# Attention and a gated MLP on one core: float32 scores for the first block alone, float16 pairs for the second block of the first batch

## The chip, the cores and the metric

One core of a Trainium2 chip runs the whole program. The metric is the device time of one execution in microseconds (us). The kernel before took 637.03 us, the median of three runs (636.49 to 640.52). One further execution was taken by the profiler; all rows come from it.

## The reference

```
scores = q @ k.T / 8, causal mask          q, k, v: 4 batches, 12 heads, 448 tokens, head size 64
attn = softmax(scores)                      (denominator + 1e-9)
x = (attn @ v), heads side by side          1792 tokens x 768
h = x @ w_in                                w_in 768 x 2048
g = h * sigmoid(1.702 h)
out = g @ w_out                             w_out 2048 x 768, everything float32
```

The inputs q and k are scaled up so that scores are far from flat, and the result has float32 accuracy. A single float16 operand isn't enough for that.

## The kernel before, in words

**Float16 pairs.** Nearly every product is made with operands split in two float16 numbers, a high part (`scaled`, L476 on ACT or L478 on DVE) and the rest (`rest`, L481, always DVE). A product is then three or four float16 matmuls that add up in PSUM. The weights come in as the high words of wider numbers: `to_f32` (L570 to L603) puts float32 together, then `split` makes the pairs (L476, L481). w_in goes through `w_in_slice` in 8 slices into `wib`, w_out through `w_out_load` and `w_out_split` in 16 pieces into `wob`.

**Blocks.** Each batch has 7 chunks of 64 tokens, cut in two blocks: chunks 0 to 3 and chunks 4 to 6. The 8 blocks are numbered n = 0 to 7; n = 0 and n = 1 belong to batch 0. A block has 6 units, a unit is two heads. `unit` makes the scores of each chunk (`scores_of`), the masked row maximum (L1091, DVE), the exponential with its row sum (L1105, ACT), reciprocal and pairs of probabilities (`p_pair`), one DMA transpose of them (L1179), the product with the values (L1197, PE) and, for two units, the pairs of the result in `xT` (L476, L481). Then `moe` takes the block: `h_slice` (L1268, PE, `xT` by `wib`, the gate on ACT and DVE into `gT`) and `out_tile` (L1333, PE, `gT` by `wob`). The out projection of n = 0 needs every piece of `wob` (16 splits at L481 on DVE).

**Two ways to scores.** `f32(b, u)` chooses. In batch 0 all units (`nf` is 6) take float32: `k_unit32` loads the keys of two heads of the block alone, `turn` transposes them on PE against an identity (L870), one copy brings them from PSUM to `kT`; `q_unit32` does the same for the queries, with two copies into `qT`; `scores32` issues one float32 matmul for a chunk, which the trace shows as two (L1060). Batches 1 to 3 take pairs: `k_pair` loads all 448 keys of four heads, takes a sum of squares (L466, ACT), the maximum over the partitions (`all_max`: L430 on PE, L632 on DVE), a power of two for scale (`norm_scale`: L443 on DVE, L450 and L457 on POOL or DVE), high part and rest into `k16`, and one DMA transpose into `kT` (L961). `q_pair` does this for the queries of four heads of a block, with sums for each partition alone, and doubles both parts (L1024, POOL); `q_unit` transposes a unit's half by DMA (L1040). `scores` issues four float16 matmuls for a chunk (L1068), each on half of the columns of the array, and L1091 then takes a scale from a column instead of a constant.

**Order.** Every step is handed to `Ops.add` with the engines that can take it, its costs, what it reads and writes, and a due time. `Ops.order` draws 300 variants of a list schedule for the whole kernel with a fixed seed, keeps the best by its own costs, and issues the instructions of each engine in that order. Loads and transposes all go through SP's queue. `keys_values` queues the keys and values of a batch two units ahead of the block that uses them.

Of the kernel before, what the change touches and what calls it, by code (L numbers as in the profile page):

```python
# [26 lines left out]
TUNE = dict(  # L27
    large=2,
    raw=(['W11', 'W11', 'V1', 'V1', 'W13', 'W15', 'W9', 'V0'], ['W11', 'W13', 'W15', 'V1', 'W15', 'V0', 'V0', 'V1']),
    tiny=True,  # L30
    win=(2, 4),
    slack=5.13,
    cuts={0: (0, 4, 7), 1: (0, 4, 7), 2: (0, 4, 7), 3: (0, 4, 7)},
    wi=(-21.7, 11.6),
    wo=(38.54, 116.08),
# [6 lines left out]
    dk=16.55,  # L42
# [2 lines left out]
    tr=26.06,  # L45
    gram_i=True,
    gram_o=False,
    nf=6,
    gram_v=True,
    va=2,  # L50
    ub=(0.0, 60.0, 122.92, 9.75),
# [8 lines left out]
class Ops:  # L60
# [24 lines left out]
    def add(self, costs, fn, r=(), w=(), prio=0.0, dma=0.0, narrow=False):  # L85
        deps = set()
        for key in r:
            if key in self.wrote:
                deps.add(self.wrote[key])
        for key in w:  # L90
            if key in self.wrote:
                deps.add(self.wrote[key])
            deps.update(self.read.get(key, ()))
        me = len(self.ops)
        for key in r:
            self.read.setdefault(key, []).append(me)
        for key in w:
            self.wrote[key] = me
            self.read[key] = []
        deps.discard(me)  # L100
        self.ops.append((costs, fn, sorted(deps), prio, dma, narrow))
# [202 lines left out]
def act(n, psum=False, ap=0, acc=0, rate=0.833):  # L304
    return {"ACT": (rate * n + (52 if psum else 94) + 93 * (ap + acc)) / 1e3}


def dve(n, ap=0, rate=1.042):
    return {"DVE": (rate * n + 68 + 61 * ap) / 1e3}
# [12 lines left out]
def kernel(  # L322
# [14 lines left out]
    NU = H // 2  # L337
# [12 lines left out]
    NB = len(blocks)  # L350
# [43 lines left out]
    add = ops.add  # L394
# [4 lines left out]
    def col(tag, n=2, w=1):  # L399
        if tag not in col_at:  # L400
            col_at[tag] = (col_used[0], Ring(n))
            col_used[0] += n * w
            assert col_used[0] <= 175
        o, ring = col_at[tag]
        i = ring.next()
        return cols[:, o + i * w : o + (i + 1) * w], ("col", tag, i)
# [424 lines left out]

    def f32(b, u):
        return b == 0 and u < TUNE["nf"]

    ident = cp.tile([P, P], F32, name="ident")
    ident_keys = ["ident"]
# [6 lines left out]
            out=ident, in_=ident, pattern=[[-1, P]], compare_op=ALU.is_equal, fill=0.0, base=0, channel_multiplier=1  # L845
        )

    if TUNE["nf"]:
        add({"POOL": 1.0}, identity, [], ident_keys, -1e6)

    def load_heads(dst, src, r, keys, prio, dma):

# [73 lines left out]
    def k_pair(b, u, prio):  # L926

        st = bst[b]
        n = 2 * S
        keys = []  # L930
        for a in range(2):
            for j in range(2):
                keys += [("kf", a, j)]
                add(
                    {"SP": Ops.LOAD},
                    lambda e, a=a, j=j: nc.sync.dma_start(
                        out=kf[64 * j : 64 * j + 64, a], in_=k[b, 2 * (u + a) + j].rearrange("(c p) d -> p c d", p=64)
                    ),
                    [], keys[-1:], prio, dma=0.64,
                )  # L940
        sq, sq_key = col("sqk", 2)
        flat = k16.rearrange("p u c g d -> p (u c g d)")
        junk_k = flat[:, :n].bitcast(BF16).rearrange("p (u c d) -> p u c d", u=2, d=D)
        square_sum(n, junk_k, [("k16", g) for g in range(2)], kf, keys, sq, sq_key, prio)
        amx, amx_key = all_max(sq, sq_key, "k", "S", prio)
        (s, s_key), (inv, inv_key) = col("s_k", 2), col("i_k", 8)
        norm_scale("k", amx, amx_key, s, s_key, inv, inv_key, prio)
        add(
            {**act(n, ap=1), **dve(n, ap=1, rate=0.521)},
            lambda e: scaled(e, k16[:, :, :, 0], kf, s),  # L950
            keys + [s_key], [("k16", 0)], prio,
        )
        add(
            dve(n, ap=1),
            lambda e: rest(k16[:, :, :, 1], kf, s, k16[:, :, :, 0]),
            keys + [s_key, ("k16", 0)], [("k16", 1)], prio,
        )
        t = kT[u // 2]
        add(
            Ops.turned(2 * NC),  # L960
            lambda e: nc.sync.dma_start_transpose(out=t, in_=flat),  # L961
            [("k16", 0), ("k16", 1)], [("kT", u + a, c) for a in range(2) for c in range(NC)], prio - TUNE["tr"], dma=2 * NC * Ops.ROWS,
        )
        for a in range(2):
            st["kT", u + a] = t[:, a * NC : a * NC + NC]
            st["ik", u + a] = inv, inv_key
# [61 lines left out]

    def q_unit(n, u, prio):
        b, c0, c1 = blocks[n]  # L1030
        if f32(b, u):
            return q_unit32(n, u, prio)
        ni = c1 - c0
        if u % 2 == 0:
            q_pair(n, u, prio)
        t, m = qT_r.next(), u % 2
        stale[t] = True
        add(
            Ops.turned(2 * ni),
            lambda e: nc.sync.dma_start_transpose(out=qT[t][:, : 2 * ni], in_=q16[:, m * 256 * ni : (m + 1) * 256 * ni]),  # L1040
            [("q16", m, g) for g in range(4)], [("qT", t)], prio - TUNE["tr"], dma=2 * Ops.ROWS * ni,
        )
        return (qT[t][:, : 2 * ni].rearrange("p (c g) t -> p g c t", g=2), ("qT", t)) + bst[b]["c", n]
# [4 lines left out]
    def scores_of(n, u, run, qt, qt_key, prio):  # L1048

        b, c0, c1 = blocks[n]  # L1050
        kt, kt_keys = bst[b]["kT", u], [("kT", u, x) for x in range(run[-1] + 1)]
        sb = ps_s_r.next()
        places, o = [], 0
        for i in run:
            places.append(ps_s[sb][:, o : o + 64 * (i + 1)])
            o += 64 * (i + 1)

        def scores32(e):
            for i, ps in zip(run, places):
                nc.tensor.matmul(  # L1060
                    ps, qt[:, i - c0].rearrange("p j w -> p (j w)"), kt[:, : 64 * (i + 1)], start=True, stop=True
                )

        def scores(e):
            for i, ps in zip(run, places):
                for g in range(2):
                    for j in range(2):
                        nc.tensor.matmul(  # L1068
                            ps[64 * j : 64 * j + 64],
                            qt[:, g, i - c0, 64 * j : 64 * j + 64],  # L1070
                            kt[:, : i + 1, 64 * j : 64 * j + 64],
                            start=(g == 0),
                            stop=(g == 1),
                        )

        if f32(b, u):
            add({"PE": (4 * o / 2.4 + 150 * len(run)) / 1e3}, scores32, [qt_key] + kt_keys, bank(sb), prio)
        else:
            add(
                {"PE": 2 * (o / 2.4 + 17 * len(run)) / 1e3}, scores, [qt_key] + kt_keys, bank(sb), prio, narrow=True  # L1080
            )
        return [(ps, [("S", sb, x)] if run[1:] else bank(sb)) for x, ps in enumerate(places)]
# [299 lines left out]
    def at(n, u):  # L1382
        p0, p1, p2, d = TUNE["ub"]
        return p0 + d * u if n == 0 else p1 + d * u if n == 1 else p2 + 10.0 * (NU * (n - 2) + u)

    AHEAD = 2

    def keys_values(n, u):
        b, c0, _ = blocks[n]
        if c0:  # L1390
            return
        if b and u == 0:
            v_batch(b, at(n, 0) - 4)
        if u % 2 == 0:
            if not f32(b, u):
                k_pair(b, u, at(n, u) - TUNE["dk"])
            v_pair(b, u, at(n, u) - (TUNE["dv"] if b else TUNE["dv0"]))

    zero_v(-1e6)
    for n, (b, c0, c1) in enumerate(blocks):  # L1400
        if c0 == 0:
            if b == 0:
                for s in range(TUNE["va"]):
                    w_in_slice(s, wi_at(s))
                v_batch(0, TUNE["v0"])
        for u in range(NU):
            if f32(b, u):
                k_unit32(u, c0, c1, at(n, u) - TUNE["dk"])
            if b == 0 and c0 == 0:
                keys_values(n, u)  # L1410
            elif n + (u + AHEAD) // NU < NB:

                keys_values(n + (u + AHEAD) // NU, (u + AHEAD) % NU)
            unit(n, u, at(n, u))
        if n == 0:
            for s in range(TUNE["va"], NWS):
                w_in_slice(s, wi_at(s))
            for nh in range(2):
                for c in range(NWS):
                    w_out_load(nh * NWS + c, TUNE["wo"][nh] + TUNE["wo1"][nh] * c)  # L1420
                w_out_scale(nh, TUNE["wo"][nh] + TUNE["wo1"][nh] * NWS)
            zero_v(TUNE["wo"][1] + TUNE["wo1"][1] * NWS)
        if n:
            moe(n - 1)
# [37 lines left out]
```

## Time and profile before

| | before |
|---|---|
| median of three runs | 637.03 us |
| the profiled execution | 634.5 us |
| its span, first to last instruction | 632.8 us |
| PE, DVE, ACT, POOL busy | 576.9, 420.2, 373.0, 98.6 us |
| matmuls | 5627 |
| mean granted TensorE clock, as a share of 2.4 GHz | 0.97 |

Busy times are averages over very different stretches. The profile has views by stretch (windows), by line and shape of tile, by what a wait was ended by, and a chain of waits that is followed back from the last instruction of a stretch. The rows that matter stand in groups below.

### The profile page before, as it was taken

To read this page: it belongs to the slowest core of one execution; us is meant where nothing else is said; L and a number is where in the kernel's file an instruction comes from. 1 tells how busy PE (TensorE), PEld (TensorE's weight loads), DVE (VectorE), ACT (ScalarE), POOL (GpSimd) and SP (SyncE) were. 2 spreads that over 40 slices of the span, in tenths; PEclk is the share of its full clock that TensorE was granted. 3 is DMA by queue.
4 is the path that set the end of the run, shared out by engine and by line. 5 is a ranking of instruction groups with operands and counts; after the bars stand their busy time and mean duration, and the time that the engine had idled before them with its cause. 6 is when DMAs were issued, how large, how long until landed. Compare 5 with 4: busy or idle time off the path is not lost.

```text
span 632.8 us, 14610 instructions
## 1 busy us (share of the span) xinstructions
PE 576.9 (91%) x5627; PEld 433.2 (68%) x5627; DVE 420.2 (66%) x1119; ACT 373.0 (59%) x869; POOL 98.6 (16%) x242
## 2 busy tenths in 40 slices
PE   4766759987999999999999999899999999999997
PEld 3554527754678768876688667785679788768864
DVE  3999899999967988997389795767674123101300
ACT  5998699998857677767477565655453213112210
POOL 2133322003411112421010520301000000000000
PEclk9867869999999999999999999999999999999999
DMA  9999869549798589899976789833850040000000
GB/s 295 257 303 296 231 220 280 148 139 185 152 182 169 111 152 154 165 148 186 171 131 125 129 181 155 138 73 63 156 100 2 14 97 1 1 26 26 2 25 26
DMA packets 226405, 85.69 MB, mean 135 GB/s; under 512 B 207136, under 2 KB 216096, under 8 KB 226336
## 3 DMA queue, kind: packets, MB, share of 16 engines
q1 hardware_dynamic: 226336, 84.76, 61.9%
q8 instruction: 44, 0.72, 0.5%
q14 instruction: 25, 0.20, 0.1%
HBM read 41.68 MB, written 5.51 MB: 75 GB/s over the span
## 4 chain that ended last, share of the span: by engine, by line
PE 50%; DVE 16%; ACT 11%; DMA 10%; issue 5%; SPq 4%; POOL 3%; DVEq 0%; ACTq 0%; POOLq 0%
PE ps_o L1333 22%; PE ps_h L1268 20%; PE ps_s L1068 3%; PE ps_v L1197 3%; DMA wob<-in_moe_w_out_dram 2%; DVE z L1091 2%; ACT z L1105 2%; SPq L981 2%; DMA qf<-in_q_dram 2%; DMA wob<-in_moe_w_in_dram 2%; DMA qT<-q 2%; DVE ps_h L1294 2%; ACT waste L466 1%; POOL cols L457 1%; PE ps_s L1060 1%
## 5 line engine op out<-in xcount | busy, mean ns | idle before, releaser
L1268 PE MATMUL ps_h<-xT,wib 128*128 128x192 f16 (+1 forms) x2304 | 233.6, 259 | 7.0 <-DVE gT L481 5.8
L1333 PE MATMUL ps_o<-wob,gT 128*128 128x384 f16 (+1 forms) x1536 | 232.9, 326 | 5.1 <-DVE wob L481 3.2
L1268 PEld LDWEIGHTS <-wib 128*128 128x128 f16 x2304 | 206.6, 98 | 32.1 <-issue 14.3
L1333 PEld LDWEIGHTS <-gT 128*128 128x128 f16 (+1 forms) x1536 | 131.1, 101 | 87.9 <-issue 10.5
L1105 ACT ACTIVATE z<-z,cols 128x320 f32<-128x320 f32 (+5 forms) x168 | 83.8, 500 | 39.7 <-DVE cols L1091 37.1
L1294 DVE SCALAR_TENSOR_TENSOR ps_h<-t,ps_h 128x512 f32<-128x512 f32 (+1 forms) x64 | 40.0, 625 | 81.1 <-ACT t L1289 80.9
L481 DVE SCALAR_TENSOR_TENSOR p<-z,cols,p 128x384 f16<-128x384 f32 (+2 forms) x168 | 82.3, 519 | 2.4 <-ACT p L476 2.0
L1289 ACT ACTIVATE t<-ps_h,cols 128x512 f32<-128x512 f32 (+1 forms) x64 | 40.1, 626 | 60.6 <-PE ps_h L1268 58.8
L1091 DVE CUSTOM_DVE_ANT_0 z<-ps_s,mask,cols 128x64 f32<-128x64 f32 (+6 forms) x126 | 55.8, 477 | 14.5 <-PE ps_s L1068 14.0
L476 ACT ACTIVATE p<-z,cols 128x128 f16<-128x128 f32 (+3 forms) x111 | 57.2, 540 | 9.3 <-DVE cols L1169 7.5
L1163 POOL TENSOR_SCALAR cols<-cols 128x2 f32<-128x2 f32 (+1 forms) x77 | 26.1, 339 | 219.9 <-ACT z L1105 219.0
L481 DVE SCALAR_TENSOR_TENSOR gT<-ps_h,gT 128x512 f16<-128x512 f32 (+1 forms) x64 | 39.7, 620 | 16.8 <-ACT gT L476 16.5
L476 ACT ACTIVATE ob<-ps_o,cols 128x384 f32<-128x384 f32 x25 | 14.4, 575 | 59.4 <-PE ps_o L1333 59.4
L476 ACT ACTIVATE gT<-ps_h 128x512 f16<-128x512 f32 (+1 forms) x57 | 30.7, 541 | 28.7 <-DVE ps_h L1294 28.4
L1197 PEld LDWEIGHTS <-v 128*64 128x64 f16 x864 | 37.8, 112 | 7.7 <-issue 5.8
L1197 PE MATMUL ps_v<-PT,v 128*64 128x192 f16 (+3 forms) x864 | 41.2, 243 | 0.8 <-DMA PT<-p 0.8
L1068 PE MATMUL ps_s<-kT,qT 128*64 128x64 f16 (+4 forms) x504 | 38.8, 277 | 2.1 <-DMA qT<-q 1.1
L1060 PE MATMUL ps_s<-kT,qT 128*128 128x64 f32 (+6 forms) x84 | 31.7, 508 | 8.2 <-DVE cols L1091 4.2
L1105 ACT ACTIVATION_READ_ACCUMULATOR z<-z,cols 128x1 f32 x168 | 31.6, 188 | 0.0
L1068 PEld LDWEIGHTS <-qT 128*64 128x64 f16 x504 | 20.5, 110 | 14.2 <-issue 10.0
L1060 PEld LDWEIGHTS ps_s<-kT,qT 128*128 128x128 f32 x84 | 16.6, 250 | 14.0 <-DVE cols L1091 7.0
L481 DVE SCALAR_TENSOR_TENSOR xT<-ps_v,xT 128x512 f16<-128x512 f32 (+1 forms) x24 | 14.8, 616 | 16.7 <-ACT xT L476 16.6
(93 smaller groups left out, 550.2 us busy)
## 6 DMA issues: line engine op xcount, KB each, us to landing
wob<-in_moe_w_in_dram SPq DMA_DIRECT2D x16, 768.0 KB, 6.4
wob<-in_moe_w_out_dram SPq DMA_DIRECT2D x9, 768.0 KB, 5.3
vraw<-in_moe_w_out_dram SPq DMA_DIRECT2D x7, 768.0 KB, 5.2
out_dram<-ob SPq DMA_DIRECT2D x28, 192.0 KB, 2.2
vraw<-in_v_dram SPq DMA_DIRECT2D x12, 384.0 KB, 5.2
kf<-in_k_dram SPq DMA_DIRECT2D x36, 112.0 KB, 3.0
qf<-in_q_dram SPq DMA_DIRECT2D x48, 64.0 KB, 2.7
qf<-in_q_dram SPq DMA_DIRECT2D x48, 48.0 KB, 2.5
```

What stands on the lines that cost most here:

```text
L476: nc.scalar.activation(out=dst, in_=src, func=AF.Copy, scale=sc)
L481: nc.vector.scalar_tensor_tensor(out=dst, in0=src, scalar=sc, in1=hi, op0=ALU.mult, op1=ALU.subtract)
L1060: nc.tensor.matmul(ps, qt[:, i - c0].rearrange("p j w -> p (j w)"), kt[:, : 64 * (i + 1)], start=True, stop=True)
L1068: nc.tensor.matmul(ps[64 * j : 64 * j + 64], qt[:, g, i - c0, 64 * j : 64 * j + 64], kt[:, : i + 1, 64 * j : 64 * j + 64], start=(g == 0), ...
L1091: lambda e: nc.vector.tensor_tensor_reduce(out=z[:, :w], in0=ps, in1=mask[:, S - w :], scale=c, scalar=3.0e38, op0=ALU.add, op1=ALU.min, a ...
L1105: lambda e: nc.scalar.activation(out=z[:, :w], in_=z[:, :w], func=AF.Exp, bias=m, scale=-1.0, accum_out=l),
L1163: lambda e, ls=ls: by(e).tensor_scalar(out=ls, in0=ls, scalar1=1e-9, scalar2=2.0**-14, op0=ALU.add, op1=ALU.mult),
L1197: nc.tensor.matmul(ps[64 * j : 64 * j + 64, 64 * (first - c0) : w], vt[:, gv, J, j, :], PT[pi][:, at, gp, 64 * j : 64 * j + 64], start=(t ...
L1268: nc.tensor.matmul(ph[:, t], wib[:, sl, u, gw, t * P : (t + 1) * P], xT[x][:, gx, u, :w], start=(u == 0 and gw + gx == 0), stop=(u == NU - ...
L1289: lambda e: nc.scalar.activation(out=th, in_=ph, func=AF.Tanh, scale=ts[:, sl : sl + 1]),
L1294: lambda e: nc.vector.scalar_tensor_tensor(out=ph, in0=th, scalar=1.0, in1=ph, op0=ALU.add, op1=ALU.mult),
L1333: nc.tensor.matmul(po[o : o + m, :OH], gT[:, f, gg, 64 * r : 64 * r + m], wo_pair(f, gw, nh), start=(f == 0 and gg + gw == 0), stop=(f == ...
```

## The change

`f32` now asks for the block alone: n = 0 keeps float32, n = 1 takes the pairs that batches 1 to 3 use. For n = 1 the second half of the keys is no longer loaded and turned by itself; instead `k_pair` makes pairs of all 448 keys, two units ahead, and puts them over the float32 keys in the same `kT` tiles. The parameter `nf` goes. All other parameters stay.

```diff
-    def f32(b, u):
-        return b == 0 and u < TUNE["nf"]
+    def f32(n):
+        return n == 0
...
-        if f32(b, u):
+        if f32(n):
             return q_unit32(n, u, prio)
...
-        if f32(b, u):
+        if f32(n):
             add({"PE": (4 * o / 2.4 + 150 * len(run)) / 1e3}, scores32, [qt_key] + kt_keys, bank(sb), prio)
...
     def keys_values(n, u):
         b, c0, _ = blocks[n]
+        if n == 1 and u % 2 == 0:
+            k_pair(b, u, at(n, u) - TUNE["dk"])
         if c0:
             return
...
-            if not f32(b, u):
+            if not f32(n):
                 k_pair(b, u, at(n, u) - TUNE["dk"])
...
-            if f32(b, u):
+            if f32(n):
                 k_unit32(u, c0, c1, at(n, u) - TUNE["dk"])
-            if b == 0 and c0 == 0:
+            if n == 0:
                 keys_values(n, u)
-            elif n + (u + AHEAD) // NU < NB:
+            if n + (u + AHEAD) // NU < NB and n + (u + AHEAD) // NU > 0:
 
                 keys_values(n + (u + AHEAD) // NU, (u + AHEAD) % NU)
```

## Rows read from the trace of the kernel before

**Rows 1.** The page: the granted clock of TensorE in 40 slices of 15.8 us (tenths of full speed).

```profile
PEclk9867869999999999999999999999999999999999
```

**Rows 2.** Busy time of each engine in six stretches (us; number of instructions in brackets), then granted clock, the DMA engines' busy share and GB/s.

```profile
0.00:92.00 92.00, 57.02 (x466) 41.61 (x467) 76.52 (x181) 74.73 (x149) 25.77 (x61) 0.80 0.94 262
92.00:132.00 40.00, 36.36 (x316) 29.16 (x316) 38.79 (x78) 36.77 (x73) 4.49 (x6) 1.00 0.80 224
132.00:150.00 18.00, 12.84 (x91) 7.12 (x89) 17.85 (x40) 17.26 (x37) 4.96 (x13) 1.00 0.80 153
150.00:180.00 30.00, 28.68 (x272) 18.51 (x271) 28.82 (x80) 22.94 (x55) 10.40 (x21) 1.00 0.86 158
180.00:240.00 60.00, 57.56 (x609) 45.38 (x609) 44.74 (x145) 41.06 (x119) 9.06 (x24) 1.00 0.77 154
240.00:633.00 393.00, 384.39 (x3884) 291.40 (x3880) 213.46 (x599) 180.23 (x441) 43.93 (x118) 1.00 0.48 91
```

**Rows 3.** The chain of waits that ends at 185 us, from 92 us on: pieces in order of time (start, us, what).

```profile
122.83 4.65 DMA wob<-in_moe_w_out_dram
127.56 1.77 ACT wob L476 x2
...
154.87 0.96 DVE wob L481
...
166.02 1.02 DVE wob L481
...
178.34 2.06 PE ps_o L1333 x12
```

**Rows 4.** The 16 splits of w_out on DVE: duration (ns, least, median, most), first and last start. Then PE's longest waits from 92 to 180 us (total, times, longest).

```profile
L481 DVE SCALAR_TENSOR_TENSOR wob<-wob,cols x16: 1005/1013/1259, 119.4 to 166.0; 128x768 f16<-128x768 f32 x16
...
PE ps_o L1333 <- DVE wob L481: 3.2, 3, 1.4
```

**Rows 5.** The float32 score matmuls (L1060) by stretch: busy us and number on PE, then on PE's weight load, clock, DMA. From 0 to 92 us they are both blocks', after it those of n = 1 alone.

```profile
0.00:92.00 92.00, 20.47 (x58) 12.65 (x58) 0.80 0.94 262
92.00:132.00 40.00, 5.99 (x14) 2.10 (x14) 1.00 0.80 224
132.00:150.00 18.00, 0.91 (x2) 0.30 (x2) 1.00 0.80 153
150.00:180.00 30.00, 4.35 (x10) 1.60 (x10) 1.00 0.86 158
```

**Rows 6.** The turns on PE (L870) after 92 us, same columns.

```profile
92.00:180.00 88.00, 1.10 (x16) 0.72 (x16) 1.00 0.82 187
```

**Rows 7.** What pairs cost on PE: all float16 score matmuls (18 units of 1792 score columns each), and the matmul of a maximum over the partitions (count, busy us, mean ns).

```profile
L1068 PE MATMUL ps_s<-kT,qT 128*64 128x64 f16 (+4 forms) x504 | 38.8, 277 | 2.1 <-DMA qT<-q 1.1
...
L430 PE MATMUL ps_s<-one,cols 128*128 128x128 bf16 x12 | 2.5, 222 | 0.9 <-ACT k L466 0.4 <-DVE cols L1091 0.4
```

**Rows 8.** DVE's operations by shape (count, busy us, mean ns, idle before): rest of keys, rest of queries, maximum of `all_max`, shift, and the row maximum with a column and with a constant for scale.

```profile
L481 DVE SCALAR_TENSOR_TENSOR k<-kf,cols,k 128x896 f16<-128x896 f32 x9 | 10.3, 1146 | 0.3 <-ACT k L476 0.2
L481 DVE SCALAR_TENSOR_TENSOR q<-qf,cols,q 128x384 f16<-128x384 f32 x9 | 6.5, 717 | 3.5 <-ACT q L476 3.5
L632 DVE TENSOR_REDUCE cols<-ps_s 128x1 f32<-128x128 f32 x12 | 3.3, 282 | 4.5 <-PE ps_s L430 4.5
L443 DVE TENSOR_SCALAR cols<-cols 128x1 int32<-128x1 int32 x41 | 5.8, 145 | 12.8 <-ACT waste L466 12.8
L1091 DVE CUSTOM_DVE_ANT_0 z<-ps_s,mask,cols 128x384 f32<-128x384 f32 x18 | 11.0, 612 | 3.2 <-PE ps_s L1068 3.0
L1091 DVE CUSTOM_DVE_ANT_0 z<-ps_s,mask 128x384 f32<-128x384 f32 x6 | 3.3, 548 | 0.0
```

**Rows 9.** ACT's operations by shape: squares of keys and queries, the read-out behind them, high parts, and the copies from PSUM of the float32 way with DVE's copy of the same shape.

```profile
L466 ACT ACTIVATE k<-kf 128x896 bf16<-128x896 f32 x9 | 8.5, 944 | 5.9 <-DMA kf<-in_k_dram 4.5 <-DMA kT<-k 1.4
L466 ACT ACTIVATE waste<-qf 128x384 bf16<-128x384 f32 x9 | 4.7, 519 | 7.8 <-DMA qf<-in_q_dram 7.6
L466 ACT ACTIVATION_READ_ACCUMULATOR k<-kf 128x1 f32 x9 | 1.7, 188 | 0.0
L476 ACT ACTIVATE k<-kf,cols 128x896 f16<-128x896 f32 x7 | 7.3, 1040 | 3.1 <-POOL cols L457 1.6 <-DVE cols L457 1.4
L476 ACT ACTIVATE q<-qf,cols 128x384 f16<-128x384 f32 x7 | 4.3, 614 | 3.6 <-DMA qT<-q 3.4
L476 ACT ACTIVATE qT<-ps_o 64x192 f32<-64x192 f32 x9 | 2.9, 319 | 0.1
L476 ACT ACTIVATE kT<-ps_o 128x192 f32<-128x192 f32 x5 | 1.6, 321 | 1.6 <-PE ps_o L870 1.6
L478 DVE TENSOR_SCALAR qT<-ps_o 64x192 f32<-64x192 f32 x3 | 1.1, 354 | 0.0
```

**Rows 10.** POOL's doubling of queries by shape (same columns).

```profile
L1024 POOL TENSOR_SCALAR q<-q 128x384 f16<-128x384 f16 x14 | 8.1, 580 | 27.0 <-ACT q L476 20.6 <-DVE q L478 3.9 <-DVE q L481 2.2
```

**Rows 11.** DMA: the hardware queue (packets, MB, share of 16 engines over the span), what HBM gave and took, and the transposes of queries and keys on SP (ns to issue one: least, median, most).

```profile
q1 hardware_dynamic: 226336, 84.76, 61.9%
HBM read 41.68 MB, written 5.51 MB: 75 GB/s over the span
...
L1040 SPq DMA_TRANSPOSE qT<-q x36: 1210/1272/2086, 159.9 to 459.1; - x36
...
L961 SPq DMA_TRANSPOSE kT<-k x9: 1579/1755/2857, 158.1 to 391.7; - x9
```

More of the change, by code (lines that the diff above doesn't have):

```diff
@@ L47 @@
     gram_o=False,
-    nf=6,
     gram_v=True,
@@ L846, in identity @@
         )
-    if TUNE["nf"]:
-        add({"POOL": 1.0}, identity, [], ident_keys, -1e6)
+    add({"POOL": 1.0}, identity, [], ident_keys, -1e6)
     def load_heads(dst, src, r, keys, prio, dma):
```

## The prediction, made before the change was run

> **What bounds the kernel now.** The page's slices of the granted clock came first: it is below full speed only in the first 100 us or so [rows 1], so PE has two lives. Then the busy time by stretches [rows 2]. From 180 us to the end PE is busy 57.56 + 384.39 = 441.95 us of about 453: there the end is set by how much work PE still has. Before that it is another kernel. From 92 to 180 us DVE is busy 38.79 + 17.85 + 28.82 = 85.5 of 88 us and ACT 77.0; from 132 to 150 us PE is idle for 5.2 of 18 us while DVE is full. The chain of waits through this stretch shows whose time it is [rows 3]: loads of w_out, then ACT and DVE on `wob`, up to a split at 166.0 us; PE heads the chain only after it, with the out projection of block 0. The splits run from 119.4 to 166.0 us, and PE's longest wait here is for them, 3.2 us in 3 times [rows 4]. So DVE and ACT set when PE gets its backlog, and PE's amount of work sets the end from about 150 us on. A price on PE counts fully only after 150 us, in part from 92 us on (PE 36.36 of 40 us), and hardly before, where PE is busy for 57.0 of 92 us and waits for others.
>
> **What goes from PE.** Block 1 has 36 float32 matmuls in the trace's count. After 92 us there are 26 of them, 5.99 + 0.91 + 4.35 = 11.25 us [rows 5], and turns of its queries, 1.10 us [rows 6]: 12.35 us. The other 10 and the remaining turns lie before 92 us, and I give them nothing, since the cover there is PE's own idle time; were PE full there, they would be worth their time as well.
>
> **What comes to PE.** Pairs cost 38.8 us for 18 units of 1792 columns [rows 7]. Block 1 has 1152 columns a unit, 64.3% of them, for 6 units: 38.8 / 3 x 0.643 = 8.3 us. Three maxima over the partitions add 3 x 0.22 = 0.7 us [rows 7]. So 9.0 us come. If all of it lands where PE is nearly full, 12.35 - 9.0 = 3.35 us are gained. If only work after 150 us counts and all pairs land there, 9.0 - 4.35 = 4.65 us are lost. If the scores keep their places, 10 of 36 after 150 us, the gain is 4.35 - 9.0 x 10/36 = 1.85 us. I take 1.9, as it follows the rows' own places; the ends stay for the range.
>
> **What comes to DVE.** For each of three groups of four heads: rest of keys 1.146, rest of queries 0.717, maximum 0.282, two shifts 0.29 us, together 2.44; three times is 7.3 us [rows 8]. The row maximum with a column for scale takes 0.612 instead of 0.548 us; 18 of them add 1.15 us. Away go 3 copies of queries and one of keys, about 4 x 0.354 = 1.4 us [rows 9]. Net +7.0 us.
>
> **What comes to ACT.** Squares 0.944 and 0.519, two read-outs of 0.188, high parts 1.040 and 0.614 us: 3.49 for a group, 10.5 us for three. Away go 9 x 0.319 + 5 x 0.321 = 4.5 us of copies [rows 9]. Net +6.0 us. The high parts may go to DVE, so I take the two engines as one pool: 13 us, 6.5 us on each if it is shared evenly.
>
> **What of it is on the path.** If nothing gives way, the last split comes 6.5 us later and so does everything behind it. Nothing at all is lost if work of batch 1, which shares DVE and ACT from 145 us on, is moved behind it: from 180 to 240 us the two are idle for 15.3 + 18.9 = 34.2 us [rows 2], and PE then has out(0) and h(1) to work on. But block 1's own softmax must come early to feed h(1). I take a third, 2.2 us, because the cover is large and lies close behind; 0 and 6.5 are the bounds.
>
> **Waits, POOL and the queues.** The new maximum waits on DVE for PE; the same reduction elsewhere sat idle 4.5 us in 12 [rows 8], so three of them are 1.1 us, from 0 to 4.5; behind them on DVE stand `wob` preparation and splits, which PE waits for. I count it within the third above. POOL's doubling adds 6 x 0.58 = 3.5 us [rows 10] and is hidden, as POOL is busy 19.9 of 88 us [rows 2]; without that cover it would be 3.5 us on the way to the queries. Loads are as many as before (12 of keys, 12 of queries), but keys grow from 48 to 112 KB each, +0.77 MB. Six transposes of queries and three of keys take SP 6 x 1.27 + 3 x 1.76 = 12.9 us to issue [rows 11], with w_out's loads, the transposes of probabilities and output stores behind them on that queue. For the DMA engines I estimate: 61.9% of 632.8 us is 392 us; 47.2 MB at the 262 GB/s of the first 92 us [rows 2] is 180 us, so transposes hold 212 us for 1,146 tiles of 128 columns (768 of probabilities, 252 of queries, 126 of keys), 0.185 us each. The change adds 3 x 14 + 6 x 6 = 78 tiles, 14.4 us, and 2.9 us for the keys: 17.4 us, where the DMA engines have 0.20 x 40 + 0.20 x 18 + 0.14 x 30 = 15.8 us free from 92 to 180 us. That just about fits; I put it at 0, with +1.6 us and what a late load makes DVE wait as the upper end, and 0 as the lower, since the turns' loads aren't fewer.
>
> Putting the pairs into `kT` must wait for block 0's scores of the same heads, which are over when block 1's begin; nothing for that.
>
> **Sum.** 634.5 - 1.9 + 2.2 = 634.8 us against the profiled execution. The median of the runs is 2.5 us above it, so 637.3, and I say 637.
>
> **Rivals.**
> *The preparation sets the end* (slower). The chain [rows 3] is DVE, ACT and loads; if block 1's pairs stand ahead of the splits, the last split slips by 6.5 us, the three waits add 1.1, the DMA engines 1.6, and PE gains nothing: 637.0 + 9.2 = 646 us. For it: DVE at 97% from 92 to 180 us, and rest operations that only DVE can take. Against: 34 us of idle time right behind. It decides if the last split begins later than about 170 us. 0.31.
>
> *PE's relief is used in full* (faster). 12.35 us less of float32 between 92 and 180 us shortens h(0) and the gaps around it; PE is idle for 3.6 + 5.2 + 1.3 = 10.1 us there [rows 2]. If 3.35 us come from work and half of the idle time goes as well, and DVE's addition hides: 637.0 - 8.4 = 628.6 us. For it: PE is the full engine of the run as a whole. Against: the idle time from 132 to 150 us waits for DVE. 0.22.
>
> *The clock falls* (a little slower). While PE was busy 62% of 0 to 92 us the granted clock was 0.80 on average, with slices at 0.6 to 0.8, so the 1.2 GHz level held part of the time [rows 1, 2]; at 36.36 of 40 us it was 1.00, which is 2.4 GHz. Without 7.1 us of float32 work, PE would have 29.3 us of work from 92 to 132 us. At 0.80 that is 36.6 us and fits; at the lower level throughout it is 58.6 us, 18.6 too many. At a clock of 0.68 it is 43, 3 us too many: about 640 us. The Trainium skill, "TensorE: Matmul & The Clock Gate", Part 1: The HAM clock gate, says that the throttled state is the default and that activity releases it; by that rule, taking work from PE can cost rate, and the sum would be some 640 instead of 637. The trace agrees in that the low clock stands only where PE was idle a third of the time. 0.05.
>
> *The order is drawn anew.* The list schedule is found for the whole kernel, so stretches without any edit change as well. After 180 us PE is idle for 453 - 442 = 11 us, and a draw can give back or take perhaps a third of it, 4 us. This is no case of its own but widens each.
>
> **How the numbers follow.** The forecast has 0.42, with a range of its own from 632 to 642 (the PE term from +3.35 to -4.65, the third from 0 to 6.5, the draw). About 1% is what a measurement of this kernel can tell from no change: below 630.7 or above 643.4. Faster by that: the faster rival but for 0.02, and 0.02 of the forecast's tail, 0.22. Slower by that: 0.27 of its rival's 0.31, and 0.05 of other tails, 0.32. Within: 0.46. The range of 8 in 10 goes from 627, where most of the faster rival lies inside, to 649, beyond the slower rival by some of its draw.
>
> **What would show it.** 26 fewer long matmuls of 128 x 128 float32 after 92 us and no turn after block 0. The splits of w_out should end at 166 to 168 us; at 172 or later the first rival holds. PE's work after 180 us should be about 442 us still; if the stretch from 132 to 150 us has no idle time on PE, the second. A granted clock under 0.9 between 92 and 132 us would be the third. Wrong altogether would be my view if block 1's scores came so late that PE, between 170 and 200 us, waits for `xT`, or if block 0, no longer sharing DVE with block 1, ended well before 92 us and h(0) began earlier.

## The result, and the profile after

The changed kernel took 644.24 us (643.75 to 645.0, three runs) against 637.03 us: 1.0106 times the time before, 95% interval 1.0073 to 1.0139. It is slower, by 7.2 us. The two profiled executions differ by more, 644.24 against 634.5 us, with spans of 642.6 and 632.8 us. Lines have moved up by one or two: the score matmuls are L1058 (float32) and L1066 (float16), the rests L480, h(.) L1266, out(.) L1331.

Busy time by stretch in the changed kernel, with the columns of [rows 2]. The DMA engines' share can pass 1.00, as the times of packets are added up there; about 1 is full.

```profile
0.00:92.00 92.00, 50.10 (x386) 37.72 (x387) 75.68 (x177) 69.68 (x142) 28.45 (x69) 0.73 1.04 258
92.00:132.00 40.00, 36.63 (x346) 28.54 (x345) 38.28 (x82) 36.79 (x71) 6.93 (x19) 0.97 1.00 256
132.00:150.00 18.00, 11.17 (x49) 4.84 (x47) 18.00 (x32) 16.32 (x32) 2.40 (x2) 0.81 1.00 216
150.00:180.00 30.00, 25.84 (x182) 15.04 (x182) 27.05 (x64) 23.14 (x50) 10.76 (x22) 0.89 0.72 130
180.00:240.00 60.00, 57.80 (x653) 44.98 (x652) 48.01 (x160) 41.85 (x124) 10.81 (x28) 1.00 0.93 166
```

The loss arises before 180 us. The next fence puts all that comes after 180 us in one row; before, PE's part of it is 57.56 + 384.39 = 441.95 us [rows 2]:

```profile
180.00:650.00 470.00, 452.69 (x4616) 342.88 (x4613) 271.62 (x787) 224.49 (x582) 57.37 (x146) 1.00 0.53 101
```

PE (TensorE) has 10.7 us more work left at 180 us. Its idle time behind that point is 642.6 - 180 - 452.69 = 9.9 us, against 10.8 us before. So PE lost the time earlier. What it waited for answers to [rows 4]:

```profile
L480 DVE SCALAR_TENSOR_TENSOR wob<-wob,cols x16: 999/1016/1399, 132.5 to 177.3; 128x768 f16<-128x768 f32 x16
```

```profile
PE ps_o L1331 <- DVE wob L480: 7.8, 8, 3.4
```

The splits of w_out begin 13.1 us later and the last one 11.3 us later (177.3 instead of 166.0); PE waits for them 8 times instead of 3. The last split begins when DVE (VectorE) has done all that stands in front of it, so its start is DVE's busy time up to there plus DVE's idle time. These are the rows up to the last split, before and then after:

```profile
0.00:166.02 166.02, 121.11 (x953) 85.83 (x955) 148.19 (x336) 141.88 (x286) 40.26 (x92) 0.89 0.87 231
```

```profile
0.00:177.28 177.28, 121.03 (x936) 84.66 (x937) 156.28 (x347) 144.77 (x290) 48.54 (x111) 0.82 0.99 234
```

So 8.1 of the 11.3 us are DVE work that now stands in front (156.28 instead of 148.19), and 3.2 us are idle time (21.0 instead of 17.8). DVE was late from the start: the first rest of w_in begins at 31.0 us instead of 20.4, the last at 100.1 instead of 86.7. Loads were late too. These are the w_in loads on SP, first before, then after (count; ns to issue; first and last start):

```profile
L652 SPq DMA_DIRECT2D wob<-in_moe_w_in_dram x16: 384/422/576, 0.8 to 61.4; - x16
```

```profile
L651 SPq DMA_DIRECT2D wob<-in_moe_w_in_dram x16: 367/426/1477, 1.3 to 74.2; - x16
```

The DMA engines' share in the rows by stretch is 1.04, 1.00 and 1.00 up to 150 us, where [rows 2] had 0.94, 0.80 and 0.80. There was room before, and there is none now.

PE's own saving never shows. Float32 scores fell from 31.7 to 15.65 us, turns from 18.6 to 10.1, and pairs rose from 38.8 to 48.5: 14.9 us less together. Yet PE's busy time is 576.4 us after 576.9. The same numbers of other matmuls have become dearer: in the page's groups h(.) went from 233.6 to 238.4 us and out(.) from 232.9 to 241.5, 13.4 us together. About half of that stands before 180 us, where the granted clock is lower than it was. Up to there one out(.) matmul takes 31.21/144 = 0.217 us of PE's time instead of 30.09/167 = 0.180, and one h(.) matmul 35.85/293 = 0.122 us instead of 36.84/315 = 0.117; by their numbers that is 5.3 and 1.6 us. Behind 180 us the clock is 1.00 in both kernels, and a single matmul lasts as long as before (326, 273 and 246 ns for the three large shapes); why the groups' busy times are larger there too is not shown.

The granted clock stands at its lower level, 1.2 GHz, in five stretches before the change, from 20.8 to 89.1 us, and in six after it, from 26.1 to 162.7 us. These are the sums over those stretches, before and then after (length, then busy time of each engine):

```profile
sum 37.50, PE 25.25 PEld 17.97 DVE 34.03 ACT 32.46 POOL 11.71; mean PE 5.05 PEld 3.59 DVE 6.81 ACT 6.49 POOL 2.34
```

```profile
sum 64.90, PE 42.87 PEld 29.54 DVE 62.60 ACT 58.95 POOL 24.36; mean PE 7.14 PEld 4.92 DVE 10.43 ACT 9.82 POOL 4.06
```

So PE did 17.6 us more of its busy time at the lower level. 12.1 us of it lie in three stretches among the splits, which begin at 138.8, 152.4 and 159.2 us. Just before each of them, at the full clock, PE was busy for 3.48 of 6.8, 2.96 of 6.8 and 1.46 of 3.4 us. The Trainium skill, "TensorE: Matmul & The Clock Gate", Part 1: The HAM clock gate, says that the throttled state is the default and activity releases it; this trace agrees: 0.81 from 132 to 150 us with PE busy 11.17 of 18 us.

### The profile page after: what moved, and what is told of

Same layout as the page of the kernel before. It is cut to its first block, busy times and chain, and to the rows that moved or that the text cites. A ratio compares the mean times of both kernels' runs of the same rounds, so it can differ in the third digit from the quotient of the medians.

```text
span 642.6 us, 14521 instructions
## 1 busy us (share of the span) xinstructions
PE 576.4 (90%) x5570; PEld 429.0 (67%) x5570; DVE 430.6 (67%) x1136; ACT 370.4 (58%) x873; POOL 105.9 (16%) x257
## 3 DMA queue, kind: packets, MB, share of 16 engines
q1 hardware_dynamic: 241984, 88.11, 65.8%
## 5 line engine op out<-in xcount | busy, mean ns | idle before, releaser
L1331 PE MATMUL ps_o<-wob,gT 128*128 128x384 f16 (+1 forms) x1536 | 241.5, 330 | 10.2 <-DVE wob L480 7.8
L1266 PE MATMUL ps_h<-xT,wib 128*128 128x192 f16 (+1 forms) x2304 | 238.4, 260 | 2.2 <-DVE gT L480 2.0
L1266 PEld LDWEIGHTS <-wib 128*128 128x128 f16 x2304 | 206.9, 98 | 30.8 <-issue 10.9
L1331 PEld LDWEIGHTS <-gT 128*128 128x128 f16 (+1 forms) x1536 | 131.7, 102 | 96.8 <-issue 25.7
L1103 ACT ACTIVATE z<-z,cols 128x320 f32<-128x320 f32 (+6 forms) x168 | 83.7, 499 | 50.1 <-DVE cols L1089 43.1
L480 DVE SCALAR_TENSOR_TENSOR p<-z,cols,p 128x384 f16<-128x384 f32 (+3 forms) x168 | 83.0, 522 | 3.7 <-ACT p L475 2.9
L1089 DVE CUSTOM_DVE_ANT_0 z<-ps_s,mask,cols 128x320 f32<-128x320 f32 (+6 forms) x144 | 66.7, 494 | 27.4 <-PE ps_s L1066 27.0
L1066 PE MATMUL ps_s<-kT,qT 128*64 128x448 f16 (+6 forms) x576 | 48.5, 287 | 5.4 <-DVE cols L1089 5.4
L1195 PEld LDWEIGHTS <-v 128*64 128x64 f16 x864 | 39.4, 115 | 16.5 <-issue 12.7
L480 DVE SCALAR_TENSOR_TENSOR gT<-ps_h,gT 128x512 f16<-128x512 f32 (+1 forms) x64 | 39.7, 620 | 14.3 <-ACT gT L475 13.8
L475 ACT ACTIVATE gT<-ps_h 128x512 f16<-128x512 f32 (+1 forms) x50 | 27.1, 542 | 23.5 <-DVE ps_h L1292 23.4
L1066 PEld LDWEIGHTS <-qT 128*64 128x64 f16 x576 | 23.0, 110 | 22.2 <-issue 19.4
L1022 POOL TENSOR_SCALAR q<-q 128x384 f16<-128x384 f16 (+1 forms) x39 | 29.5, 760 | 39.7 <-ACT q L475 26.0
L475 ACT ACTIVATE wob<-wob 128x768 f32<-128x768 f32 (+1 forms) x20 | 21.8, 1089 | 15.0 <-DMA wob<-in_moe_w_in_dram 12.9
L456 POOL TENSOR_SCALAR cols<-cols 128x1 int32<-128x1 int32 x34 | 11.7, 343 | 77.7 <-DVE cols L442 68.6
```

The lines of the kernel that those rows point to most:

```text
L475: nc.scalar.activation(out=dst, in_=src, func=AF.Copy, scale=sc)
L480: nc.vector.scalar_tensor_tensor(out=dst, in0=src, scalar=sc, in1=hi, op0=ALU.mult, op1=ALU.subtract)
L1022: nc.gpsimd.tensor_scalar(out=dst, in0=src, scalar1=1.0, scalar2=1.0, op0=ALU.mult, op1=ALU.mult)
L1066: nc.tensor.matmul(ps[64 * j : 64 * j + 64], qt[:, g, i - c0, 64 * j : 64 * j + 64], kt[:, : i + 1, 64 * j : 64 * j + 64], start=(g == 0), ...
L1089: lambda e: nc.vector.tensor_tensor_reduce(out=z[:, :w], in0=ps, in1=mask[:, S - w :], scale=c, scalar=3.0e38, op0=ALU.add, op1=ALU.min, a ...
L1103: lambda e: nc.scalar.activation(out=z[:, :w], in_=z[:, :w], func=AF.Exp, bias=m, scale=-1.0, accum_out=l),
```

## The experiments

All ratios are to the kernel before, run on the same chip. Each trace is one execution. The runs whose names begin with f_ or r_ leave out or replace work of block 1, so its scores aren't the right ones; they are there for their time alone.

| run | what it is | ratio, 95% interval | us | last split of w_out | PE work after 180 us | DMA share to 150 us |
|---|---|---|---|---|---|---|
| before | | 1 | 637.0 | 166.0 | 442.0 | 0.89 |
| after | | 1.0106 [1.0073, 1.0139] | 644.2 | 177.3 | 452.7 | 1.02 |
| before_s2 | before, second draw | 0.9954 [0.9922, 0.9987] | 636.5 | 164.8 | 442.5 | 0.90 |
| before_s10 | before, third draw | 1.0077 [1.0051, 1.0103] | 644.7 | 171.2 | 448.9 | 0.95 |
| after_s2 | after, second draw | 1.0142 [1.0116, 1.0168] | 648.7 | 175.0 | 450.7 | 1.06 |
| after_s7 | after, third draw | 1.0107 [1.0087, 1.0127] | 645.8 | 179.6 | 451.2 | 1.01 |
| f_no_tr | after's order, no transposes | 1.0094 [1.0055, 1.0133] | 645.2 | 177.4 | 452.9 | 0.91 |
| f_copy | after's order, copies | 1.0075 [1.0051, 1.0100] | 644.2 | 174.6 | 451.1 | 0.94 |
| f_no_vec | after's order, no preparation | 1.0120 [1.0074, 1.0166] | 647.0 | 174.3 | 453.2 | 1.00 |
| f_both | after's order, neither | 1.0032 [1.0007, 1.0057] | 641.4 | 169.8 | 448.0 | 0.93 |
| r_no_tr | redrawn, no transposes | 1.0093 [1.0065, 1.0121] | 643.6 | 170.0 | 447.9 | 0.93 |
| r_no_tr_s2 | the same, second draw | 1.0011 [0.9981, 1.0040] | 638.8 | 171.7 | 445.0 | 0.93 |
| r_no_vec | redrawn, no preparation | 1.0114 [1.0068, 1.0160] | 645.6 | 171.1 | 450.5 | 1.04 |
| r_no_vec_s2 | the same, second draw | 1.0179 [1.0144, 1.0214] | 649.4 | 173.6 | 453.5 | 1.00 |
| r_no_both | redrawn, neither | 0.9974 [0.9945, 1.0004] | 635.6 | 168.7 | 441.9 | 0.97 |
| r_no_both_s2 | the same, second draw | 1.0051 [1.0022, 1.0081] | 642.5 | 168.4 | 445.7 | 0.94 |
| plan_free_dma | after, another plan | 1.0129 [1.0076, 1.0183] | 645.9 | 180.7 | 455.0 | 1.01 |
| dose1 | pairs for units 4, 5 alone | 0.9972 [0.9946, 0.9998] | 637.4 | 169.9 | 444.4 | 0.94 |
| dose2 | pairs for units 2 to 5 | 1.0010 [0.9980, 1.0041] | 638.8 | 171.5 | 445.0 | 1.00 |
| dose_first | pairs for units 0, 1 alone | 1.0020 [1.0000, 1.0041] | 639.0 | 173.9 | 447.6 | 0.93 |

**Is it a matter of the drawn order?** Four runs change the seed alone.

```diff
-SEED = 1
+SEED = 2
```

> The kernel before with another seed for its order, nothing else. If the loss of 7.2 us is chance in the drawn order, before with another seed should scatter by as much: some 640 to 648 us here. If the loss belongs to the pairs themselves, this stays within about 4 us of 637.

> The kernel before with a third seed. Chance in the order: anywhere from 634 to 650 us. Loss belongs to the pairs: below 643.

> The changed kernel with another seed. Chance in the order: as likely below 637 as above it. Loss belongs to the pairs: 641 to 651 us, above every run of the kernel before.

> The changed kernel with a third seed. Chance in the order: about 637 give or take 7. Loss belongs to the pairs: 641 to 651 us, with DMA engines full (share near 1.0) up to 150 us as in the changed kernel.

Hardly by chance alone. Three draws of the change lie at 1.011 to 1.014, three of before at 0.995 to 1.008, and all three above all three comes out by chance once in 20. But before_s10, at 644.7 us, lies above the bound of 643 that I had set for a loss that belongs to the pairs, and the draw is worth as much as many an edit: from one seed to another the kernel before moved by 1.2%, and its worst draw falls short of the change by only 0.3%. Any redrawn run below is read against a scatter of about 0.6% to either side.

**Which of the added work costs?** To keep the draw out, the next runs leave the order, each instruction's engine and place, as it is in the changed kernel, and only don't issue some of it. Where the transposes or the preparation are missing, other instructions read the value tiles in place of the missing result, or scales set once beforehand; the cuts show only what is left out. Without the nine transposes:

```diff
-            lambda e: nc.sync.dma_start_transpose(out=t, in_=flat),
+            lambda e: nc.sync.dma_start_transpose(out=t, in_=flat) if b else None,
...
-            lambda e: nc.sync.dma_start_transpose(out=qT[t][:, : 2 * ni], in_=q16[...]),
+            lambda e: nc.sync.dma_start_transpose(out=qT[t][:, : 2 * ni], in_=q16[...]) if n != 1 else None,
```

> The changed kernel with every instruction in its place, except that block 1's nine DMA transposes (three of keys, six of queries) are not issued and its scores read the value tiles instead, so the scores of block 1 are not computed. If the transposes' time on the DMA engines and in SP's queue makes the loss: 636 to 639 us, and the last split of w_out starts 5 us or more before 177. If the work added to DVE and ACT makes it: within 2 us of 644. If the order makes it: also within 2 us of 644.

With plain copies of the same bytes in their place (`nc.sync.dma_start` between the same tiles):

> The changed kernel in its own order, with block 1's nine transposes replaced by plain copies of the same bytes between the same tiles (block 1's scores are wrong by that). The waits of the chain stay. If it is the transposes' time on the DMA engines: between the run without them and 644, about 640. If it is the wait for them: 644.

Without block 1's preparation:

```diff
+    def mute(i0):
+        for i in range(i0, len(ops.ops)):
+            o = ops.ops[i]
+            ops.ops[i] = (o[0], lambda e: None) + o[2:]
...
+        if b == 0:
+            mute(n0)
         t = kT[u // 2]
```

> The changed kernel in its own order, without block 1's preparation on ACT, DVE, POOL and PE (squares, maxima, scales, high parts, rests, doubling); loads and transposes stay, the transposes read the value tiles. If the 13 us on DVE and ACT make the loss: 637 to 640 us. If the transposes make it: 642 to 644. If the order: 644.

And without both:

> The changed kernel in its own order, with block 1's transposes and its preparation on ACT, DVE, POOL and PE both left out (its scores are not computed). If the two resources cover for each other and the order isn't at fault: 634 to 638 us, as in the redrawn run without both. If the loss is now in the places of the other steps: 641 us or more, though less work is left than in the kernel before.

Neither omission alone gives the time back; both together give 4.7 us of 6.8 (1.0032 against 1.0106). If the two merely added up, both together would stand at 1.0108; they stand 0.8% below that, where the four intervals together leave some 0.7%. The rows up to the last split say how. Columns as in [rows 2]; without transposes, then without preparation, then without both:

```profile
0.00:177.42 177.42, 120.21 (x936) 83.89 (x937) 156.17 (x348) 145.18 (x290) 48.92 (x111) 0.82 0.89 220
```

```profile
0.00:174.31 174.31, 117.92 (x933) 83.42 (x934) 150.33 (x333) 136.79 (x272) 36.34 (x91) 0.82 0.98 238
```

```profile
0.00:169.76 169.76, 118.12 (x933) 83.10 (x934) 149.45 (x333) 137.00 (x272) 40.42 (x91) 0.83 0.91 230
```

Without transposes the DMA engines have room again (0.91 up to 150 us), but DVE has the same list of work in the same order and is as busy as ever (156.17 us); the last split begins at 177.4 us as if nothing had been taken away. Without preparation the DMA engines are as full as before. DVE has 5.9 us less to do before the last split, but 3.0 us of that turn into idle time (24.0 instead of 21.0), and the last split comes 3.0 us earlier. These are single traces: f_copy, with 155.8 us of work on DVE, is idle for 18.8 us, so 2 us of idle time are little evidence. Without both, DVE has 6.8 us less to do and is idle for 20.3 us, and the last split begins at 169.8 us.

Who waits for whom changes over as well. Without transposes the loads of w_out wait on SP for buffers that DVE and ACT (ScalarE) still hold: 27.1 us up to 150 us by the three longest waits; in the changed kernel the same three come to 7.0 us, and to 28.1 in the kernel before:

```profile
SPq L703 <- ACT wob L465: 12.1, 5, 5.5
SPq L703 <- DVE wib L480: 7.7, 3, 5.3
SPq L703 <- ACT vraw L465: 7.3, 3, 3.5
```

Without preparation it is ACT that waits longer for weights to land, 20.2 us instead of 14.9 (6.7 in the kernel before).

All this fits two full resources in front of the splits, each of which covers for the other. It isn't the whole loss: f_both missed the 634 to 638 us that were forecast for that, and came out at the 641 us forecast for a loss by the places of the other steps. By its ratio some 2 us are left, though it has less work than the kernel before. The copies keep the waits and move the same bytes in (0.94 - 0.91) x 150 = 4.5 us of the DMA engines' time, and they gain 2 us or nothing by their interval. No run takes the DMA engines' time away and leaves SP the time to issue the transposes, so the two aren't told apart.

**Can another order use what is freed?** Here the work is left out before the order is drawn. The cut is against the runs above.

```diff
-            Ops.turned(2 * NC),
+            Ops.turned(2 * NC) if b else {"SP": 0.02},
...
-            ops.ops[i] = (o[0], lambda e: None) + o[2:]
+            ops.ops[i] = (o[0] if "SP" in o[0] else {"POOL": 0.005}, (o[1] if "SP" in o[0] else lambda e: None)) + o[2:]
```

> Block 1's nine transposes are left out before the order is drawn, and its scores read the value tiles (block 1's scores are not computed). In the changed kernel's own order leaving them out gave nothing, so now: if the loss is that the order is built around their time on SP and the DMA engines, 636 to 640 us; if DVE and ACT's added work is the loss, 643 to 648; if the chain of four heads at once through single buffers is, 643 to 648 too.

> Second draw of the redrawn run without block 1's transposes (its scores are not computed). If neither omission alone recovers the time: 643 to 649 us. If the first draw was an unlucky one: 636 to 641.

> Block 1's preparation on ACT, DVE, POOL and PE is left out before the order is drawn; loads and transposes stay, the transposes read the value tiles (block 1's scores are wrong by that). If DVE and ACT's 13 us are the loss: 636 to 640 us, with the last split of w_out before 170. If the transposes or the buffers are: 643 to 649.

> Second draw of the redrawn run without block 1's preparation on ACT, DVE, POOL and PE. If neither omission alone recovers the time: 643 to 649 us. If the first draw was an unlucky one: 636 to 641.

> Both are left out before the order is drawn; the loads and the float16 score matmuls of block 1 stay (its scores are not computed). Transposes or vector work: 630 to 638 us, as PE also has less to do than before. If it stays at 643 or more, the loss is in neither: loads, or the way the units hang together.

> The redrawn run without transposes and without preparation, with the seed that gave 648.7 us for the full change. If leaving out both is what recovers the time: 633 to 640 us again. If the first such run was a lucky draw: 641 to 648.

Against the change's mean of 1.012, the mean without preparation is 1.015, without transposes 1.005, without both 1.001. So preparation alone is worth nothing in any of three runs, and both together are worth about 1% in either draw, 1.3 and 0.9 (though r_no_both_s2, at 642.5 us, missed its 633 to 640). The transposes alone are the less clear case: 1.0093 fits the forecast of no gain, 1.0011 that of a full one, and the difference between them is hardly more than a draw's width. That r_no_vec and r_no_vec_s2 keep the DMA engines full (1.04, 1.00) and stay slow would fit if the DMA engines come first, but that isn't shown, and how much the transposes alone would give back isn't settled.

**Does the plan merely shy away from a cost?** The order is drawn as if block 1's transposes took the DMA engines no time.

```diff
-dma=2 * NC * Ops.ROWS,
+dma=2 * NC * Ops.ROWS if b else 0.0,
...
-dma=2 * Ops.ROWS * ni,
+dma=2 * Ops.ROWS * ni if n != 1 else 0.0,
```

> The changed kernel with all its work; only the order is drawn as if block 1's transposes took no time on the DMA engines (SP's part stays). If the order shies away from a cost that the chip doesn't have: 637 to 641 us. If the transposes really take the DMA engines' time: 644 to 650. If DVE and ACT's work is the loss: 643 to 648.

It doesn't: 1.0129, the latest last split of all (180.7 us), and the DMA engines at 1.01. At 645.9 us the run fits both other forecasts, 644 to 650 for the transposes' time and 643 to 648 for the work on DVE and ACT, so it doesn't tell them apart.

**How does it grow?** Pairs for a part of block 1's units, float32 for the others.

```diff
-    def f32(n):
-        return n == 0
+    def f32(n, u=0):
+        return n == 0 or n == 1 and u < 4
```

> Float32 for block 0 and for the first four units of block 1; pairs for its last two units alone, one third of the change. If the loss grows with the work (DVE, ACT, DMA engines together): 637 to 641 us. If it comes from the first pair being there at all (buffers shared with block 0's staging): 643 or more.

> Pairs for the last four units of block 1, two thirds of the change. Loss grows with the work: 640 to 645 us, between the run with a third and the full change. Otherwise as the run with a third.

> Pairs for the first two units of block 1 alone, float32 for its other four: one third of the change, as dose1, but the third whose preparation falls into the first 75 us, where the DMA engines are full. If the early place makes the loss: 642 to 646 us. If the amount makes it, growing more than in proportion: 636 to 640, as dose1.

Perhaps not in proportion: either third that was tried is free within the draw (0.9972 late, 1.0020 early), two thirds are still free at 1.0010 (638.8 us, where a loss that grows with the work was forecast at 640 to 645), and all three cost 1.1%. But each is a single draw. In proportion two thirds would cost 0.7%, and the draw's 0.6% just about covers the distance, so this isn't settled. The early place isn't the reason, as dose_first shows. The DMA share up to 150 us goes 0.94, 1.00, 1.02. dose2 at 1.00 without loss and f_no_tr at 0.91 with it say that the share alone doesn't decide; the order on DVE does its part.

**What goes with the time over all twenty?** The start of the last split does so only roughly: r_no_tr_s2, dose2 and dose_first begin it at 171.5 to 173.9 us and lose 0.1 to 0.2%, while r_no_tr begins it at 170.0 and loses 0.9%. PE's work after 180 us does better: it is 447.9 us or more for every ratio from 1.0075 up, and 448.0 or less for every lower one.

The fastest kernels that compute everything are before_s2 and dose1. Neither beats the kernel before by more than a draw does.

## Why the prediction was wrong

- **What bounds the kernel** held: splits of w_out that come late, and PE's work after them. The splits' end told the two kernels apart (177.3 against a bound of 170 to 172 us); over the other runs that bound doesn't hold, and PE's work after 180 us, forecast at 442 us and measured at 452.7, is the better sign.
- **PE's 1.9 us of gain** isn't there. The amounts were near: all 26 float32 matmuls after 92 us are gone, and pairs cost 9.7 us where I had 8.3. But PE now waits 7.8 us for splits where it waited 3.2, and of the 13.4 us by which the same matmuls became dearer about half is the lower clock's.
- **DVE +7.0, ACT +6.0** came out as +10.4 (430.6 us) and -2.6 (370.4), +7.8 us in sum instead of 13. The sum was too high, but none of it went to ACT.
- **"I take a third, 2.2 us"** is the step that failed. I held that batch 1's work would give way. The last split slipped by 11.3 us, beyond even my upper bound of 6.5 us: 8.1 us by DVE work in front of it, more than the whole 7.0 that I had for DVE, and 3.2 us by idle time. Both rows that I had for the cover, DVE and ACT idle from 180 to 240 us, were true, and much of that time is still idle (12.0 and 18.2 us); it wasn't used. There was little to move: one rest of batch 1's keys stood in front of the last split, and one still does, now with three of block 1's. Why the drawn order puts all of block 1's preparation first is open.
- **"That just about fits; I put it at 0"** failed with it. The price of the transposes was near: f_no_tr puts them at (1.02 - 0.91) x 150 = 16.5 us, where I had 14.4. The change as a whole takes (1.02 - 0.89) x 150 = 19.5 us up to 150 us, where I had 17.4, but over the whole span 31 us (65.8% of 642.6 us against 61.9% of 632.8). Of that 14 us stay without the transposes (63.0% of 643.9 us), and their cause is open. And I set demand against the free time of 92 to 180 us as if all of it could be used in any order. In the changed kernel the nine transposes are issued from 70.0 to 136.3 us, four of them before 92 us, where the share had been 0.94 already.
- **The first rival** was nearest: 646 us forecast, 644.2 measured. I gave it 0.31. Its sign and place are right, late splits that keep PE from its work. That its number is so near is in part luck: it added 6.5, 1.1 and 1.6 us, where the last split alone slipped by 11.3, and by the experiments its two parts cover for each other, so that they aren't to be added.
- **The clock** as a rival fell: 0.97 from 92 to 132 us, where I had put it. It is lower from 132 to 180 us, behind PE's waits, and before 92 us, where PE has less work than before (0.73 after 0.80).
- **The draw** widened each case by 4 us; measured, it is 8 us from 636.5 to 644.7 for the same kernel before.

## What to carry to other kernels

Before moving work off the engine that is fullest over the run, look at which engines are full in the stretch where that work stands: here DVE and the DMA engines, whose work PE waited for, got more to do so that PE had less. When two resources are both full in a stretch, taking load off one can show nothing, so a null result of such an experiment doesn't acquit it; take both away, and keep the order fixed. Where a scheduler redraws the whole order, measure several draws of the kernel before first; here one draw is worth up to 1.2%.

## What the runs showed of the hardware

The nine transposes (78 tiles of 128 x 128 float16, 2.56 MB) took 16.5 us of all 16 DMA engines (f_no_tr against after), 0.21 us a tile, some 155 GB/s. Plain copies of the same bytes between the same tiles took 4.5 us (f_copy against f_no_tr). And 14.9 us less work on PE left PE's busy time as it was, with 42.9 us of it at the 1.2 GHz level where it had been 25.3: a busy time can hide a saving. The clock accounts for about half of the 13.4 us by which other matmuls became dearer; the rest isn't explained.
